# Softmax-weight transposes on VectorE and through DRAM in a fused attention and feed-forward kernel

## The chip, the cores and the metric

One core of one Trainium2 chip runs the whole program. The metric is device microseconds (us) of one execution, as the median of several runs.

## What is computed

The reference, cut to its arithmetic (q, k and v are 4 batches x 8 heads x 768 positions x 64, float32; n_sink = 4, window = 128; w_in is 512 x 2048, w_out 2048 x 512):

```
keep = (key < n_sink) | ((0 <= query - key) & (query - key < window))
scores = q @ k.T / 8, and -1e9 where not keep
a = exp(scores - rowmax); a = a / (sum(a) + 1e-9)
x = a @ v, heads put side by side: 3072 tokens x 512
h = x @ w_in; g = h - tanh(h); out = g @ w_out
```

## The kernel before

The 3072 tokens are cut into 12 chunks of 256 (three per batch). A chunk's attention is done in four **units**, one for each pair of heads, so there are 48 units, u = 0 to 47, and unit u belongs to chunk u // 4. A unit's steps, with the tile names that the profile shows:

- `split` (L471 on): ScalarE and VectorE cut keys and queries into a high and a low part (tiles `ks` and `q`). The first 12 units skip it.
- `scores` (L504 on), once for each half t of the chunk's 256 queries: four matmuls of 260 columns into tile `s` (L523). `s` has one buffer, so that the second half has to wait until VectorE has read the first (`merge`: L535 and L541), which writes the packed scores `p`. A query sees 4 sink keys and 128 keys of the band, so a row of `p` is 132 wide. ScalarE takes the exponential (L549).
- `normalise`: VectorE makes the reciprocal sums (L569, L570), ScalarE scales the four rows (L575), GpSimd copies out the sink columns (`z`).
- `turn` (L593 on): TensorE turns the four 128 x 128 blocks of weights (two heads by two halves) against the identity, into PSUM tile `t` (L602). VectorE multiplies them into tile `pt` twice, once by the mask `below` (keys of the query's own block) and once by `after` (keys of the block before): two operations over 512 columns at L616. In the first chunk of a batch they are 256 wide, and ScalarE makes a plain copy beside them (L609).
- `attend` (L625 on), once per chunk from chunk 3 on: TensorE turns the sink weights (L633), ScalarE copies them (`zr`), and 2 + 24 matmuls build `x`, the chunk's attention output, from `pt` and the values `v` (L650, L656). ScalarE and VectorE split `x` into `xh` and `xl`.

The feed-forward part has 96 **steps**: 12 chunks by 8 groups of 256 hidden columns. Step n is a block h(n) of 24 matmuls (L730), a gate on ScalarE and VectorE (tanh L735, difference L738, cast to `gh` L742, rest to `gl` L746), and a block o(n) of 12 matmuls (L778), 8 of them with `gh` and then 4 with `gl`. `h` has two PSUM buffers. The weights are loaded once, early, and decoded on VectorE and ScalarE (L165 to L169, L703, L708).

**What sets the order.** The engines run in the order in which `Work.order` (L216 on) lists the jobs. Each job has an engine, an estimated duration, a due time and the resources that it reads and writes. A list scheduler gives every engine, whenever it is free, the ready job that is due first. SyncE (SP), which issues the DMAs, is planned in the same way: one queue, in order. On TensorE `rank` bends this rule from step 23 on: a started block is finished first, and after an o block an h block goes ahead of anything else:

```python
if last[0] == "o":
    return (0 if b and b[0] == "h" else 1, due, n)
```

So attention work enters TensorE's order only behind an h block. The due time of a unit (`due_unit`) is that of its chunk's first step less `LEAD` = 24000 ns and less 14400 ns for each unit that follows it in the chunk; a gate is due with its step. The first matmul of an h block is written with a reordered access pattern where the block before it is not h (`_pieces`, L178: pieces of 16 elements).

Of the kernel before, what the change touches and what calls it, by code (L numbers as in the profile page):

```python
# [9 lines left out]
F32 = mybir.dt.float32  # L10
# [176 lines left out]
class Work:  # L187
# [28 lines left out]
    def order(self):  # L216
        todo = {}
        for n, (engine, *_) in enumerate(self.all):
            todo.setdefault(engine, []).append(n)
        users, left = [[] for _ in self.all], [len(t[4]) for t in self.all]  # L220
        for n, t in enumerate(self.all):
            for a in t[4]:
                users[a].append(n)
        ready = {n: 0.0 for n, k in enumerate(left) if k == 0}
        waiting = {e: [n for n in v if n in ready] for e, v in todo.items()}
        free, port, start, done = dict(self.BEGIN), {}, {}, {}
        parts, last = {}, None
        for b in self.block:
            parts[b] = parts.get(b, 0) + 1

        def rank(n):

            b, due = self.block[n], self.all[n][2]
            if last is None or last[1] < FREE or self.all[n][0] != "PE":
                return (1, due, n)
            if parts[last]:
                return (0 if b == last else 1, due, n)
            if last[0] == "o":
                return (0 if b and b[0] == "h" else 1, due, n)
            return (1, due, n)  # L240

        def at(n, e):
            t = max(free[e], ready[n])
            return max(t, port.get("DVE" if e == "POOL" else "POOL", 0.0)) if self.all[n][6] else t

        while any(waiting.values()):
            t, e = min((min(at(n, e) for n in v), e) for e, v in waiting.items() if v)
            n = min((n for n in waiting[e] if at(n, e) <= t), key=rank)
            if self.block[n]:
                last = self.block[n]  # L250
                parts[last] -= 1
            _, took, _, _, _, lands, locks = self.all[n]
            waiting[e].remove(n)
            start[n], free[e], done[n] = t, t + took, t + took
            if lands:
                free[e], done[n] = t + lands, t + lands + self.LANDING
            if locks:
                port[e] = t + took
            for u in users[n]:
                f = self.all[u][0]  # L260
                lag = 0 if f == e else self.WAKE[e] + (self.SLACK if f == "PE" else 0)
                ready[u] = max(ready.get(u, 0.0), done[n] + lag)
                left[u] -= 1
                if not left[u]:
                    waiting[f].append(u)
        return sorted(start, key=lambda n: (start[n], n)), start


def _banded(tc, qd, kp, vp, vs, masks, w_in, w_out, ident, pts, early, out):
    nc = tc.nc  # L270
    et = mybir.EngineType
    with ExitStack() as ctx:

        def pool(name, bufs, **kw):
            return ctx.enter_context(tc.tile_pool(name=name, bufs=bufs, **kw))
# [5 lines left out]
        qpool, vpool, hpool = pool("qpool", 2), pool("vpool", 3), pool("hpool", 1)  # L281
        xpool, gpool = pool("xpool", 2), pool("gpool", 2)
        spool, pp, sm = pool("spool", 1), pool("pp", 2), pool("sm", 4)
        ps_s, ps_t, ps_x = pool("ps_s", 1, space=PSUM), pool("ps_t", 1, space=PSUM), pool("ps_x", 1, space=PSUM)
        ps_h, ps_o = pool("ps_h", 2, space=PSUM), pool("ps_o", 1, space=PSUM)
        work, before = Work(), {}


        RAW, TWO, CUT, DUO, PB, ZL, TK = 12, 12, 1, 3, 4, 0, 1100

        chunks = [(b, 0) for b in range(3)] + [(b, c) for b in range(3) for c in range(1, CPB)]
        chunks += [(b, c) for b in range(3, B) for c in range(CPB)]
# [2 lines left out]
        order += [(cc, g) for g in range(CUT, NG) for cc in (2, 1)] + [(0, g) for g in range(CUT, NG)]  # L295
        order += [(cc, g) for cc in range(3, NCHUNK) for g in range(NG)]
        NS = len(order)
        FIRST, EARLY, PACE, LEAD = 55000.0, 4600.0, 7200.0, 24000.0
        UNIT, SECOND, WLEAD, WNEXT = 2600.0, 1000.0, 6000.0, 1500.0

        def due_step(n):
# [288 lines left out]
        def place(u):  # L590
            return u % 2 if u < DUO * NPAIR else u % NPAIR

        def turn(u):  # L593
# [28 lines left out]
            work.add("DVE", 430 if c == 0 else 710, d + 1500, lambda: part(1, below), ["t"], [("pt own", m)])  # L622
            work.add("DVE", 430 if c == 0 else 710, d + 1500, lambda: part(0, after), ["t"], [("pt before", m)])

        def attend(cc, p0, pairs):  # L625

            b, c = chunks[cc]
            key, banks = (cc, p0), range(pairs // 2)

            def sink_rows():  # L630
                xps[key] = [ps_x.tile([P, 2, CH], F32, tag="x", name=f"x{cc}_{p0}")]
                for t in range(2):
                    nc.tensor.transpose(  # L633
                        xps[key][0][:, 1, t * P : (t + 1) * P],
                        zt[:, t].bitcast(F32).rearrange("p n a b c -> p (n a b c)"), ident,
                    )

            def sink_copy(m):

                nc.scalar.activation(zr[:, m, :], xps[key][0][:, 1, :], AF.Copy, scale=odd[:, m : m + 1])  # L640

            def values():
                if pairs == NPAIR:
                    ps = ps_t.tile([P, 2, 2, P], F32, tag="t", name=f"x{cc}_2")
                    xps[key].append(ps.rearrange("p a b q -> p a (b q)"))
                plan = [(2 * c, 0, CH, 1), (2 * c + 1, P, CH, 3)]
                if c > 0:
                    plan.append((2 * c - 1, 0, P, 0))
                for i in banks:
                    nc.tensor.matmul(xps[key][i], lhsT=vsink[:, p0 // 2 + i], rhs=zr, start=True, stop=False)  # L650
                for p in range(p0, p0 + pairs):
                    for n, (i, a, z, blk) in enumerate(plan):
                        for h in range(2):
                            rhs = pts[:, place(NPAIR * cc + p), h].rearrange("p a b -> p (a b)")[:, blk * P : blk * P + z - a]
                            hd = (2 * p + h) * D
                            nc.tensor.matmul(  # L656
                                xps[key][(p - p0) // 2][h * 64 : h * 64 + 64, p % 2, a:z],
                                lhsT=vt[cc, i][:, hd : hd + D], rhs=rhs,
                                start=False, stop=p % 2 == 1 and n == len(plan) - 1,
                            )  # L660

            def x_high(i):
                if p0 == 0 and i == 0:
                    where, a, b = (hpool, "hb", "ha") if home(cc) == 2 else (xpool, "xh", "xl")
                    xh[cc] = where.tile([P, NPAIR, CH], F32R, tag=a, name=f"xh{cc}")
                    xl[cc] = where.tile([P, NPAIR, CH], F32R, tag=b, name=f"xl{cc}")
                r = slice(p0 + 2 * i, p0 + 2 * i + 2)
                nc.scalar.copy(xh[cc][:, r, :], xps[key][i])

            def x_low(i):  # L670
                r = slice(p0 + 2 * i, p0 + 2 * i + 2)
                nc.vector.tensor_tensor(xl[cc][:, r, :], xps[key][i], xh[cc][:, r, :].bitcast(F32), op=ALU.subtract)

            last = NPAIR * cc + p0 + pairs - 1
            d = due_unit(last) + 5500
            work.add("PE", 230, d + 1500, sink_rows, [("z", i) for i in range(NPAIR)], ["x"])
            for m in range(2):
                work.add("ACT", 270, d + 2000, lambda m=m: sink_copy(m), ["x"], [("zr", m)])
            v = [vslot[cc, i] for i in range(max(0, 2 * c - 1), 2 * c + 2)]
            pt = [(f"pt {k}", place(NPAIR * cc + i)) for k in ("whole", "own", "before") for i in range(p0, p0 + pairs)]  # L680
            need = pt + ["vsink", ("zr", 0), ("zr", 1)] + v
            work.add("PE", (340 + 735 * pairs if c == 0 else 200 + TK * pairs), d + 3500, values, need, ["x", "t"][: pairs // 2])
            for i in banks:
                x = [("xu", home(cc), p0 + 2 * i), ("xu", home(cc), p0 + 2 * i + 1)]
                work.add("ACT", 490, d + 5000, lambda i=i: x_high(i), ["xt"[i]], x + [("x", home(cc))] * (p0 + i == 0))
                work.add("DVE", 690, d + 5200, lambda i=i: x_low(i), ["xt"[i]], x)
# [45 lines left out]
        def gate(n):  # L732
# [12 lines left out]
                gl[n] = gpool.tile([P, 2, CH], F32R, tag="gl", name=f"gl{n}")  # L745
                nc.vector.tensor_tensor(gl[n], hps[n], gh[n].bitcast(F32), op=ALU.subtract)  # L746

            d, h, r = due_step(n), ("h", n % 2), n % 2
            work.add("ACT", 510, d, tanh, [h], ["gr"])
            work.add("DVE", 705, d, difference, ["gr"], [h])  # L750
            work.add("ACT", 526, d, high, [h], [("gh", r)])
# [80 lines left out]
        def attention(cc):  # L832
            if cc and chunks[cc][0] != chunks[cc - 1][0]:
                sink_values(chunks[cc][0], due_unit(NPAIR * cc) + 4000)
            for u in range(NPAIR * cc, NPAIR * cc + NPAIR):
                if not raw(u):
                    split(u)
                for t in range(2):
                    scores(u, t)
                if RAW <= u + 2 < NU:  # L840
                    load_qk(u + 2)
                normalise(u)
                turn(u)
                if cc < DUO and u % 2:
                    attend(cc, u % NPAIR - 1, 2)
            if cc >= DUO:
# [244 lines left out]
```

## Time and profile before

| | |
|---|---|
| three runs, median (lowest to highest) | 679.7 us (679.7 to 679.93) |
| the profiled execution's own time | 680.06 us |
| its span, first to last instruction | 678.3 us |
| busy: TensorE, VectorE, ScalarE, GpSimd | 664.6, 426.7, 368.0, 51.1 us |
| mean granted TensorE clock | 0.999 of full speed |

A busy time is the sum over the stretches in which the engine had at least one instruction under way. Matmuls overlap each other: the mean duration of one is longer than the distance from one start to the next, so the pace of TensorE is read from the starts. "Idle before" names the engine or the transfer whose end released the waiting instruction.

### The profile page before, as it was taken

To read this page: it belongs to the slowest core of one execution; us is meant where nothing else is said; L and a number is where in the kernel's file an instruction comes from. 1 tells how busy PE (TensorE), PEld (TensorE's weight loads), DVE (VectorE), ACT (ScalarE), POOL (GpSimd) and SP (SyncE) were. 2 spreads that over 40 slices of the span, in tenths; PEclk is the share of its full clock that TensorE was granted. 3 is DMA by queue.
4 is the path that set the end of the run, shared out by engine and by line. 5 is a ranking of instruction groups with operands and counts; after the bars stand their busy time and mean duration, and the time that the engine had idled before them with its cause. 6 is when DMAs were issued, how large, how long until landed. Compare 5 with 4: busy or idle time off the path is not lost.

```text
span 678.3 us, 12421 instructions
## 1 busy us (share of the span) xinstructions
PE 664.6 (98%) x4604; PEld 592.8 (87%) x4604; DVE 426.7 (63%) x1084; ACT 368.0 (54%) x1001; POOL 51.1 (8%) x201
## 2 busy tenths in 40 slices
PE   7999999999999999999999999999999999999996
PEld 5777899999989989989989998998998998998995
DVE  6889999947945556656655665565555656564221
ACT  5996433447845565455455655556556456553222
POOL 6220000000000010000001000001000000000000
PEclk9999999999999999999999999999999999999999
DMA  6789800012121022012103112112013102100001
GB/s 207 246 266 385 337 1 5 0 62 84 56 75 45 28 83 82 28 59 68 48 28 110 52 32 90 29 55 92 27 30 100 45 28 60 59 1 1 32 1 36
DMA packets 31712, 52.13 MB, mean 77 GB/s; under 512 B 3228, under 2 KB 21020, under 8 KB 31644
## 3 DMA queue, kind: packets, MB, share of 16 engines
q1 hardware_dynamic: 31340, 50.93, 22.8%
q8 instruction: 38, 0.62, 0.4%
q10 hardware_dynamic: 304, 0.33, 0.2%
q14 instruction: 30, 0.25, 0.1%
HBM read 44.96 MB, written 6.29 MB: 76 GB/s over the span
## 4 chain that ended last, share of the span: by engine, by line
PE 90%; ACT 3%; DVE 3%; SPq 1%; issue 1%; POOL 1%; DMA 1%; POOLq 0%; ACTq 0%
PE o L778 39%; PE h L730 37%; PE s L523 5%; PE x L656 5%; PE t L602 2%; ACT p L575 1%; ACT p L549 1%; PE x L650 1%; DMA qk<-kp 1%; DVE p L541 0%; DVE pt L167 0%; PE x L633 0%; DVE pt L169 0%; SPq L106 0%; DVE pt L616 0%
## 5 line engine op out<-in xcount | busy, mean ns | idle before, releaser
L730 PE MATMUL h<-xh,w 128*128 128x256 f32 x1536 | 279.9, 278 | 0.0
L730 PEld LDWEIGHTS h<-xh,w 128*128 128x128 f32 x1536 | 239.1, 188 | 3.3
L730 PE MATMUL h<-xl,w 128*128 128x256 f32 x768 | 212.5, 277 | 0.0
L778 PE MATMUL o<-w,gh 128*128 128x512 f32 x768 | 194.6, 394 | 0.6 <-ACT gh L742 0.6
L778 PEld LDWEIGHTS o<-w,gh 128*128 128x128 f32 x768 | 137.2, 188 | 26.4 <-ACT gh L742 1.0
L730 PEld LDWEIGHTS h<-xl,w 128*128 128x128 f32 x768 | 144.2, 188 | 3.2
L735 ACT ACTIVATE graw<-h 128x512 f32<-128x512 f32 x96 | 57.4, 598 | 157.5 <-PE h L730 157.2
L778 PE MATMUL o<-w,gl 128*128 128x512 f32 x384 | 103.9, 391 | 0.0
L549 ACT ACTIVATE p<-p,st 128x132 f32<-128x132 f32 x192 | 76.0, 398 | 48.3 <-DVE st L541 47.9
L746 DVE TENSOR_TENSOR gl<-h,gh 128x512 fp32r<-128x512 f32 x96 | 66.2, 690 | 46.7 <-ACT gh L742 46.5
L738 DVE TENSOR_TENSOR h<-h,graw 128x512 f32<-128x512 f32 x96 | 66.9, 696 | 40.5 <-ACT graw L735 39.4
L535 DVE COPY_PREDICATED s<-above,s 128x256 f32<-128x256 uint32 x80 | 33.9, 424 | 92.6 <-PE s L523 92.4
L778 PEld LDWEIGHTS o<-w,gl 128*128 128x128 f32 x384 | 71.7, 188 | 15.4
L742 ACT CAST gh<-h 128x512 fp32r<-128x512 f32 x96 | 56.2, 586 | 30.3 <-DVE h L738 30.2
L575 ACT ACTIVATE p<-p,st 128x132 f32<-128x132 f32 x192 | 62.1, 396 | 7.2 <-DVE st L570 7.0
L541 DVE CUSTOM_DVE_ANT_0 p<-s,mask 128x132 f32<-128x132 f32 x192 | 48.9, 292 | 8.2 <-POOL qraw L374 2.4
L523 PE MATMUL s<-ks,q 128*128 128x260 f32 x288 | 49.7, 295 | 0.0
L580 POOL CAST z<-p 128x16 fp32r<-128x16 f32 x48 | 10.2, 212 | 500.8 <-ACT p L575 498.9
L616 DVE TENSOR_TENSOR pt<-t,below 128x512 f32<-128x512 f32 (+1 forms) x48 | 28.8, 601 | 30.3 <-PE t L602 29.0
L485 DVE TENSOR_TENSOR ks<-kraw,ks 64x392 fp32r<-64x392 f32 x72 | 40.4, 561 | 5.7 <-ACT ks L480 3.5
L656 PE MATMUL x<-pt,v 128*64 128x128 f32 (+1 forms) x512 | 41.5, 315 | 0.0
L656 PEld LDWEIGHTS x<-pt,v 128*64 128x64 f32 x512 | 31.0, 137 | 11.7 <-issue 4.8
(77 smaller groups left out, 547.4 us busy)
## 6 DMA issues: line engine op xcount, KB each, us to landing
qraw<-qd SPq DMA_DIRECT2D x36, 256.0 KB, 2.7
wraw<-w_in SPq DMA_DIRECT2D x16, 512.0 KB, 7.2
wraw<-w_out SPq DMA_DIRECT2D x16, 512.0 KB, 8.2
kraw<-kp SPq DMA_DIRECT2D x37, 196.0 KB, 2.4
v<-vp SPq DMA_DIRECT2D x27, 256.0 KB, 2.7
out<-ob SPq DMA_DIRECT2D x24, 256.0 KB, 2.3
qk<-kp SPq DMA_DIRECT2D x8, 196.0 KB, 4.9
qk<-qd SPq DMA_DIRECT2D x16, 64.0 KB, 4.8
```

Of the source, the lines that this page charges most:

```text
L485: nc.vector.tensor_tensor(k[o, h, :], t[r, :], k[r, h, :].bitcast(F32), op=ALU.subtract)
L523: nc.tensor.matmul(ps[h][:, :WIN], lhsT=q[:, h, t * P : (t + 1) * P], rhs=rhs, start=i == 0, stop=i == 1,)
L541: nc.vector.tensor_tensor_reduce(out=pr[u][:, j, :], in0=ps[h][:, P:WIN], in1=mask[:, kind, :], scale=-0.125, scalar=BIG, op0=ALU.add, op1 ...
L549: nc.scalar.activation(e, e, AF.Exp, bias=st[u][:, j : j + 1], scale=-1.0, accum_out=st[u][:, 4 + j : 5 + j],)
L575: nc.scalar.activation(pr[u][:, j, :], pr[u][:, j, :], AF.Copy, scale=s[:, 8 + j : 9 + j])
L656: nc.tensor.matmul(xps[key][(p - p0) // 2][h * 64 : h * 64 + 64, p % 2, a:z], lhsT=vt[cc, i][:, hd : hd + D], rhs=rhs, start=False, stop=p ...
L730: nc.tensor.matmul(y, lhsT=w, rhs=x, start=r == 0, stop=r == 11)
L735: nc.scalar.activation(gr[n], hps[n], AF.Tanh)
L738: nc.vector.tensor_tensor(hps[n], hps[n], gr[n], op=ALU.subtract)
L742: nc.scalar.copy(gh[n], hps[n])
L746: nc.vector.tensor_tensor(gl[n], hps[n], gh[n].bitcast(F32), op=ALU.subtract)
L778: nc.tensor.matmul(ops[cc, t], lhsT=(gh, gh, gl)[i][n][:, f, t * P : (t + 1) * P], rhs=wt[1, g][:, (0, 1, 0)[i], f, :], start=first and no ...
```

## The change

From chunk 4 on (units 16 to 47; `APART` = 16) `turn_apart` takes the place of `turn`. VectorE transposes the four blocks in squares of 32 x 32 (`squares`) into one half of `pt`. SyncE writes that half, 128 rows of 2 KB, to a DRAM buffer (`away`) and reads it back in four transfers of 32 partitions, in runs of 512 bytes, so that each square comes to its place (`back`), into the other half of `pt`. VectorE then multiplies by `after` into the first half (`not_own`: two operations of 8 x 32 columns, one in the first chunk of a batch) and by `below` in place (`only_own`: 512 columns, or 256). `attend` reads the columns of `pt` through `weight_columns`, in runs of 32 elements that lie 128 elements apart. Units 0 to 15 keep the old way.

Three numbers of the planner change besides: the rule of `rank` that is quoted above goes away, so that attention may follow an o block as well; `LEAD` is 42000 ns in place of 24000; gates are due 12000 ns earlier from step 20 on.

```diff
-            if last[0] == "o":
-                return (0 if b and b[0] == "h" else 1, due, n)
+        dram = pool("dram", 4, space=bass.MemoryType.DRAM)
-        FIRST, EARLY, PACE, LEAD = 55000.0, 4600.0, 7200.0, 24000.0
+        FIRST, EARLY, PACE, LEAD = 55000.0, 4600.0, 7200.0, 42000.0
+        def weight_columns(m, h, blk):
+            v = pts[:, m].rearrange("p h b q -> p (h b q)").rearrange("p (r h t j) -> p r h t j", h=2, t=2, j=32)
+            return {1: v[:, :, h, 0], 3: v[:, :4, h, 1], 0: v[:, 4:, h, 1]}[blk]
+        def turn_apart(u):
...
+            def squares():
+                dst = other.rearrange("p b h t j -> p (h t) b j")
+                nc.vector.transpose(dst, pr[u][:, :, NSK:].rearrange("p n (b j) -> p n b j", j=32))
+            def away():
+                dt[0] = dram.tile([P, 4 * P], F32, tag="turned", name=f"turned{u}")
+                nc.sync.dma_start(dt[0], other.rearrange("p b h t j -> p (b h t j)"))
+            def back():
+                rows = dt[0].rearrange("(a i) (b e) -> b i a e", a=4, b=4)
+                dst = own.rearrange("p a h t j -> p a (h t j)")
+                for b in range(4):
+                    nc.sync.dma_start(dst[32 * b : 32 * b + 32], rows[b])
...
+            def not_own():
+                for t in range(c == 0, 2):
+                    masked(other[:, :, :, 1 - t], own[:, :, :, t], after)
+            def only_own():
+                v = own[:, :, :, 1] if c == 0 else own.rearrange("p a h t j -> p a (h t) j")
+                masked(v, v, below)
...
+            work.add("DVE", 620, d, squares, ps, before)
+            work.add("SP", 500, d + 800, away, before, [("turned", u % 4)], lands=800)
+            work.add("SP", 1500, d + 4200, back, [("turned", u % 4)], mine + [("pt whole", m)], lands=1500)
+            work.add("DVE", took if c == 0 else 760, d + 8000, not_own, mine, before, port=True)
+            work.add("DVE", took, d + 8000, only_own, (), mine, port=True)
...
+                            if NPAIR * cc + p >= APART:
+                                rhs = weight_columns(place(NPAIR * cc + p), h, blk)
...
-            d = due_unit(last) + 5500
+            d = due_unit(last) + (5500 if NPAIR * cc < APART else 9500)
...
-            d, h, r = due_step(n), ("h", n % 2), n % 2
+            d, h, r = due_step(n) - (12000.0 if n >= 20 else 0.0), ("h", n % 2), n % 2
...
-                turn(u)
+                (turn if u < APART else turn_apart)(u)
```

**TensorE, around step 42 or 43, before.** L602 are the transposes, L523 the scores, L778 an o block, L730 the first matmuls of the next h block:

```order
L602 MATMUL t<-ident,p 128x128 x4
L523 MATMUL s_0<-ks,q 128x260 x4
L778 MATMUL o<-w_2,gh 128x512 x8
L778 MATMUL o<-w_2,gl 128x512 x4
L730 MATMUL h<-xh,w_4 128x4x4x16
```

**TensorE there with the change.** Line numbers are those of the changed file: L522 scores, L687 the turned sink rows, L834 o, L786 h:

```order
L522 MATMUL s_0<-ks,q 128x260 x4
L687 MATMUL x_0<-ident,z 128x128 x2
L834 MATMUL o<-w_3,gh 128x512 x8
L834 MATMUL o<-w_3,gl 128x512 x4
L522 MATMUL s_1<-ks,q 128x260 x4
L834 MATMUL o<-w_4,gh 128x512 x8
L834 MATMUL o<-w_4,gl 128x512 x4
L786 MATMUL h<-xh,w_5 128x4x4x16
```

The transposes are gone. Before, each o block was followed by an h block, and the two halves of a unit's scores had an h and an o block between them; now they stand one o block apart, o(43) and o(44) follow each other with only scores between them, and h(43) and h(44) stood together ahead of them.

**VectorE, around one unit, before.** L738 and L746 are the gate's difference and `gl`, L616 the two masked copies out of PSUM, L535 and the ISA rows the merge of the scores:

```order
L738 TENSOR_TENSOR h<-h,graw 128x512
L746 TENSOR_TENSOR gl<-h,gh 128x512
L616 TENSOR_TENSOR pt<-t,below 128x4x128
L616 TENSOR_TENSOR pt<-t,after 128x4x128
L535 COPY_PREDICATED s_0<-above,s_0 128x2x128
L541 ISA p,st<-s_0,mask 128x132
```

**VectorE around one unit with the change.** L492 and L484 are the low parts of queries and keys, L659 the masks, L794 and L802 the gate, L644 the squares:

```order
L492 TENSOR_TENSOR q<-qraw,q 128x512
L659 TENSOR_TENSOR pt<-pt,after 128x8x32 x2
L659 TENSOR_TENSOR pt<-pt,below 128x512
L568 TENSOR_SCALAR st<-st 128x4
L569 RECIPROCAL st<-st 128x4
L484 TENSOR_TENSOR ks<-kraw,ks 64x392
L794 TENSOR_TENSOR h<-h,graw 128x512
L484 TENSOR_TENSOR ks<-kraw,ks 64x392
L644 STREAM_TRANSPOSE pt<-p 128x4x4x32
L802 TENSOR_TENSOR gl<-h,gh 128x512
```

The masks of one unit stand ahead of the squares of the next, and both stand in the queue that the gate's difference and `gl` use.

**SyncE around one chunk's end, with the change.** L648 is `away`, L654 `back`, L851 the store of the output, L365 and L354 the loads of queries and keys:

```order
L648 DMA turned<-pt 128x512
L654 DMA pt<-turned 32x4x128 x4
L851 DMA out<-ob_0 128x512
L851 DMA out<-ob_1 128x512
L365 DMA qraw<-qd 128x2x256
L354 DMA kraw<-kp 128x392
L648 DMA turned<-pt 128x512
L654 DMA pt<-turned 32x4x128 x4
```

Before, the queue held only the loads and the stores there. Each unit now puts a write and four reads between them, the reads waiting for the write.

## Rows read from the trace of the kernel before

**Rows 1.** Busy time in stretches: us, PE, PEld, DVE, ACT, POOL, clock, DMA share, GB/s.

```profile
85.00:102.00 17.00, 17.00 (x115) 15.53 (x113) 16.86 (x20) 6.53 (x10) 0.00 (x0) 1.00 0.00 1
...
221.00:238.00 17.00, 17.00 (x114) 15.48 (x114) 10.34 (x31) 9.52 (x27) 0.63 (x3) 1.00 0.09 28
```

**Rows 2.** TensorE's waits over the span: us in total, times, longest us.

```profile
PE o L778 <- ACT gh L742: 0.6, 2, 0.3
```

**Rows 3.** TensorE's timeline: start us, us, line, operation, count.

```profile
201.16 0.28 PE L730 MATMUL h<-xh,w 128*128 128x256 f32 x1
201.27 0.28 PE L730 MATMUL h<-xl,w 128*128 128x256 f32 x1
...
203.90 0.64 PE L523 MATMUL s<-ks,q 128*128 128x260 f32 x4
204.38 2.02 PE L778 MATMUL o<-w,gh 128*128 128x512 f32 x8
...
215.87 0.60 PE L602 MATMUL t<-ident,p 128*128 128x128 f32 x4
216.23 0.73 PE L523 MATMUL s<-ks,q 128*128 128x260 f32 x4
216.80 2.00 PE L778 MATMUL o<-w,gh 128*128 128x512 f32 x8
...
240.68 0.60 PE L602 MATMUL t<-ident,p 128*128 128x128 f32 x4
241.11 0.38 PE L633 MATMUL x<-ident,z 128*128 128x128 f32 x2
241.25 0.72 PE L523 MATMUL s<-ks,q 128*128 128x260 f32 x4
241.81 2.01 PE L778 MATMUL o<-w,gh 128*128 128x512 f32 x8
...
245.12 3.69 PE L656 MATMUL x<-pt,v 128*64 128x256 f32 x48
```

**Rows 4.** Groups by shape: count | busy us, mean ns of one | idle before.

```profile
L602 PE MATMUL t<-ident,p 128*128 128x128 f32 x192 | 29.4, 275 | 2.5 <-DVE pt L616 1.2 <-ACT p L575 0.8 <-ACT pt L609 0.4
L616 DVE TENSOR_TENSOR pt<-t,below 128x512 f32<-128x512 f32 x32 | 22.1, 691 | 26.5 <-PE t L602 26.5
```

**Rows 5.** Timeline of TensorE and ScalarE, one half of a unit: scores, then the scaled rows.

```profile
263.96 0.64 PE L523 MATMUL s<-ks,q 128*128 128x260 f32 x4
...
267.32 1.30 ACT L575 ACTIVATE p<-p,st 128x132 f32<-128x132 f32 x4 [0.25 <-DVE st L570]
```

**Rows 6.** DMA issues by tile: count, KB each, median us to landing; and the queue's line.

```profile
q1 hardware_dynamic: 31340, 50.93, 22.8%
...
qraw<-qd SPq DMA_DIRECT2D x36, 256.0 KB, 2.7
...
out<-ob SPq DMA_DIRECT2D x24, 256.0 KB, 2.3
```

**Rows 7.** SyncE's timeline of the early stretch: start us, us, line, transfer, count.

```profile
66.46 2.86 SPq L401 DMA_DIRECT2D v<-vp  x3
```

**Rows 8.** VectorE's timeline, the first decoding operation of w_in's group 5.

```profile
100.81 0.69 DVE L165 TENSOR_SCALAR pt<-wraw 128x1024 uint32<-128x1024 uint32 x1
```

**Rows 9.** The chain that ended last, two h blocks (88, 89) and o(88).

```profile
629.00 5.46 PE h L730 x48
634.47 2.74 PE o L778 x12
```

**Rows 10.** ScalarE's timeline, the gate of step 88: tanh, then `gh`.

```profile
631.84 0.60 ACT L735 ACTIVATE graw<-h 128x512 f32<-128x512 f32 x1 [1.73 <-PE h L730]
633.21 0.59 ACT L742 CAST gh<-h 128x512 fp32r<-128x512 f32 x1 [0.77 <-DVE h L738]
```

**Rows 11.** Timelines of TensorE and ScalarE, step 41: h(41) ends with L602's start; `gh`.

```profile
257.55 0.60 PE L602 MATMUL t<-ident,p 128*128 128x128 f32 x4
...
261.04 0.57 ACT L742 CAST gh<-h 128x512 fp32r<-128x512 f32 x1
```

More of the change, by code (lines that the diff above doesn't have):

```diff
@@ L286, in _banded @@
         work, before = Work(), {}
-        RAW, TWO, CUT, DUO, PB, ZL, TK = 12, 12, 1, 3, 4, 0, 1100
+        RAW, TWO, CUT, DUO, PB, ZL, TK, APART = 12, 12, 1, 3, 4, 0, 1100, 16
         chunks = [(b, 0) for b in range(3)] + [(b, c) for b in range(3) for c in range(1, CPB)]
@@ L623, in turn, with halves @@
             work.add("DVE", 430 if c == 0 else 710, d + 1500, lambda: part(0, after), ["t"], [("pt before", m)])
+        def halves(m):
+            v = pts[:, m].rearrange("p h b q -> p (h b q)").rearrange("p (o a h t j) -> p o a h t j", o=2, a=4, h=2, t=2)
+            return v[:, 1], v[:, 0]
+        def weight_columns(m, h, blk):
+            v = pts[:, m].rearrange("p h b q -> p (h b q)").rearrange("p (r h t j) -> p r h t j", h=2, t=2, j=32)
+            return {1: v[:, :, h, 0], 3: v[:, :4, h, 1], 0: v[:, 4:, h, 1]}[blk]
@@ new lines, in turn_apart, with masked @@
+        def turn_apart(u):
+            cc, p, b, c = unit(u)
+            m = place(u)
+            other, own = halves(m)
+            dt = {}
+            def squares():
[9 more added lines that the diff above has]
+                    nc.sync.dma_start(dst[32 * b : 32 * b + 32], rows[b])
+            def masked(dst, src, mask):
+                z = list(src.shape)
+                mask = mask.rearrange("p (a j) -> p a j", j=32).unsqueeze(2).to_broadcast(z)
+                nc.vector.tensor_tensor(dst, src, mask, op=ALU.mult)
+            def not_own():
[4 more added lines that the diff above has]
+                masked(v, v, below)
+            d = due_unit(u) + 5500
+            ps = [("p", slot(u), 0), ("p", slot(u), 1)]
+            took = 430 if c == 0 else 710
+            before, mine = [("pt before", m)], [("pt own", m)]
+            work.add("DVE", 620, d, squares, ps, before)
[3 more added lines that the diff above has]
+            work.add("DVE", took, d + 8000, only_own, (), mine, port=True)
```

## The prediction

> **What bounds the kernel now.** I read the busy time by stretches first. From 85 us on TensorE is busy for all 17.00 us of every 17, and its clock is granted in full (1.00) [rows 1]. The other engines are not full in the steady part: VectorE has 10.34 and ScalarE 9.52 of 17 us. VectorE is full only early (16.86 of 17 at 85 to 102 us), while it decodes weights [rows 1]. The list of TensorE's waits says the same from the other side: for the gate's result `gh` it waited 0.6 us in the whole run, in two places [rows 2]. So after the start the time is the sum of TensorE's blocks, and what leaves TensorE leaves the time, unless a new wait comes in. The price of a block is read in TensorE's timeline, as the distance from its start to the next start [rows 3].
>
> **What the change takes off TensorE.** Units 16 to 47 lose their transposes: 32 units, four each. Four transposes start at 215.87 us and the scores behind them at 216.23, so 0.36 us. They also make the next block slower: those scores take 216.80 - 216.23 = 0.57, where scores behind an h block take 204.38 - 203.90 = 0.48. A unit thus loses 0.36 + 0.09 = 0.45 us [rows 3]. In eight of the 32, one per chunk, the turned sink rows (L633) stand between transposes and scores. These sink rows stay, are the same kind of matmul and keep the slower block behind them, so only about 0.36 goes. The stretch there, from 240.68 to 241.81, is 1.13 us for the three [rows 3]. Sum: 24 x 0.45 + 8 x 0.36 = **13.7 us**.
>
> The mean duration of a transpose in the list of groups is 275 ns [rows 4], and 128 of them would be 35.2 us. That is the wrong column: they overlap, and four take 0.36 us from start to start. The Trainium skill (TensorE: Matmul & The Clock Gate, "Part 4: PE-mode transpose") gives about 275 ns for a transpose in a kernel's context and 390 ns alone. By that figure the saving would again be an estimated 35 us, and the pace in this trace contradicts it.
>
> **What it adds to TensorE.** The 24 matmuls of each x block now read weights in runs of 32 elements. The trace has a nearer case than the plain one: the first matmul of an h block reads pieces of 16 elements and starts its successor after 201.27 - 201.16 = 0.11 us, the pace of a plain one [rows 3]. I take 0. The other end would be half pace in all eight x blocks, 8 x 3.6 = 29 us (the block of 48 passes from 245.12) [rows 3].
>
> **VectorE.** Two masked operations per unit, 691 ns each [rows 4], become squares, one or two half-wide masks and one full mask. None of these shows in the trace. The nearest row is the same 691 ns for 512 columns, and I take that for each 512: three in place of two, 0.7 us more per unit and 32 x 0.7 = 22 us in about 450. That raises 10.34 of 17 to about 11.2 [rows 1]. VectorE does not become the bound. If the squares cost twice as much, it is 11.9. At the low end masks out of SBUF are cheaper and the load stays as it is. ScalarE loses four plain copies.
>
> **SyncE and the DMAs.** Each unit adds one write of 256 KB and four reads of 64 KB. The page's queue line gives 22.8% of 16 engines over 678.3 us for 31340 packets, 79 ns a packet [rows 6]. A unit adds 128 packets of 2 KB and 512 of 512 bytes, so 640 x 0.079 / 16 = 3.2 us of DMA time, against about 13 us between units (eight steps of 5.5 us and the attention blocks make a chunk of over 50): cover enough. The nearest write, `out`, lands in 2.3 us, and a read of as many bytes (`qraw`) in 2.7 [rows 6]. For the four reads the ends are 2.7 (side by side) and 10.8 (one after the other). Three issues in a row took 2.86 us at most [rows 7], so the last of four is issued no more than about 2.9 us after the first, and 2.7 + 2.9 = 5.6 bounds them if they overlap. I take 4.2, nearer to side by side.
>
> The in-order queue is also moved early on: loads for chunk 3 (`kraw`, `qraw`, `vraw`, three `v`) now stand ahead of the weight groups 4 and 5. The `v` loads wait for a buffer until 66.46 us and end at 69.32 [rows 7], so group 5 starts behind them. VectorE first needs it at 100.81 [rows 8], 31 us later, more than ten times what a load of 256 KB takes [rows 6]. That costs nothing.
>
> **Is x ready in time?** With the changed order I count the blocks on TensorE between a chunk's last scores and its x block: 17.6 us in five chunks, 16.6 in one, 14.9 in two (h and o 2.74 each, scores 0.48) [rows 3, 9]. What has to fit: scores end to scaled weights, 264.4 to 268.6, is 4.2 us with its queueing [rows 5]; squares 0.7; write 2.3; reads 4.2; masks 1.4; some five handoffs of 0.1. Sum 13.3 us, 14.7 with the reads at 5.6. It fits, with little to spare in two chunks.
>
> **Are the gates ready in time?** This is where I expect what the change gives back. Before, an h and an o block, 5.5 us or more, nearly always lay between the end of h(n) and the start of o(n). In the changed order I count 34 steps from 27 to 87 with only 2.74 to 4.15 us. A gate with nothing in its way takes from 631.73 (h(88) ends halfway through 5.46 us from 629.00) to 633.80 (the end of `gh`), 2.1 us, and 2.2 with the handoff [rows 9, 10]; its 2.74 us of cover were enough. A gate in a full queue took much longer: h(41) ended at 257.55 and its `gh` at 261.61, 4.1 us [rows 11]. Over the counted steps, waits sum to 0 us if a gate needs 2.2 us, 1.7 at 3.2, 7.3 at 3.5 and 22.3 at 4.1. I take 0.8, a need of about 3.0. The planner puts o(n) where its own estimate has the gate done, and the order that it made from the same estimates before, in which x blocks too were placed as soon as they were due, left TensorE waiting 0.6 us for `gh` [rows 2].
>
> **Sum.** 680.06 - 13.7 + 0.8 = 667.2 us against the profiled execution's own time (span 678.3 to 665.4). That execution is 0.36 above the median of 679.7, so the forecast is **666.8 us**.
>
> **The rivals.**
> - *The gates wait a little* (a need of 3.5 us): 679.7 - 13.7 + 7.3 = 673.3. For it: three VectorE operations more stand in the gate's queue, and the scores' merges must fit behind a single o block. Against: the earlier due times put gates ahead. Chance 0.19.
> - *The gates wait as at step 41*, slower than before. Place: o(n) directly behind the previous o block. Price: 679.7 - 13.7 + 22.3 = 688.3. It turns the sign from a mean need of about 3.75 us on. Against: at step 41 the planner had 5.5 us or more and no reason to hurry. Chance 0.06.
> - *The round trip is late.* If the four reads land one after the other (10.8 us), the chain is 19.9 us, and x waits 5 x 2.3 + 3.3 + 2 x 5.0 = 24.8 us: 690.8. It turns the sign from reads of about 9 us on. Against: 16 engines share the packets. Chance 0.05. The Trainium skill (VectorE: DVE Perf Modes, "The three transpose paths") warns that a plain copy which transposes by its strides is 19 times slower than the DMA's own transpose where the innermost step is large. By that factor the reads would take an estimated 80 us, and x would hold every chunk. Here the innermost run is 512 bytes long, not a single element, and no row before shows such a copy.
> - *Runs of 32 halve TensorE's pace*: 679.7 - 13.7 + 29 = 695.0, chance 0.03, with the 0.11 us against it [rows 3].
> - *The listed mean is what leaves*: 679.7 - 35.2 = 644.5, chance 0.01.
> - *Nothing is left*: the waits happen to take about what the transposes gave. Chance 0.02.
>
> The forecast itself, with waits of up to 4 us (665.6 to 670), keeps 0.64.
>
> **Range and chances.** A measurement of this kernel tells about 0.2%, 1.4 us. The range goes from 664.8 (0.45 us saved at the eight sink places too, 14.4 in all, and scores that follow an o block a little cheaper) up to 675, past the first rival; the slower cases, 0.14 together, are left out, with the few others. Faster: 0.64 + 0.19 + 0.01 = 0.84; same 0.02; slower 0.14.
>
> **What would show it.** L602 falls from 192 to 64 matmuls and the stretches from 200 us on stay at 17.00 of 17, with chunks about 1.7 us shorter than before. TensorE's waits show at most a few microseconds for `gh` or for `s`, and none for `pt`. The squares and masks last 0.4 to 0.8 us each, and VectorE stays near 11 of 17. The reads land within about 4 us. I am wrong if TensorE has holes behind o blocks (the gate), ahead of x (the round trip) or behind the first half of the scores (the merge), or if the x block takes more than 3.7 us.

## The result, and the profile after

The changed kernel takes 667.83 us (median of four runs, beside 679.79 us for the kernel before): a ratio of 0.9822, 95% interval 0.9803 to 0.9841. One of the four runs took 1319.9 us, which no other run here came near, and is left out of the ratio; the other three took 667.43 to 668.03 us. The forecast was 666.8 us, in a range of 664.8 to 675. The profiled execution took 667.43 us, its span is 665.7 us, 12.6 less than before.

The page after, busy times (us, share of the span, instructions):

```profile
PE 652.5 (98%) x4476; PEld 580.9 (87%) x4476; DVE 450.8 (68%) x1144; ACT 367.3 (55%) x997; POOL 54.7 (8%) x201
```

Busy time by stretches after, columns as in [rows 1]:

```profile
85.00:102.00 17.00, 17.00 (x115) 15.53 (x114) 16.11 (x21) 6.43 (x9) 0.00 (x0) 1.00 0.11 36
...
221.00:238.00 17.00, 17.00 (x117) 15.57 (x115) 12.21 (x35) 10.43 (x32) 1.75 (x6) 1.00 0.30 86
```

TensorE is still full in every one of the stretches of 17 us that I read between 85 and 646 us. VectorE has 12.21 of 17 us in the stretch from 221 us, and 11.30 in the mean of those stretches, where it had 10.50 before. TensorE's wait for `gh` in the list of waits, then the same two waits in its timeline:

```profile
PE o L834 <- ACT gh L798: 0.6, 2, 0.3
```

```profile
60.82 1.20 PE L834 MATMUL o<-w,gh 128*128 128x512 f32 x4 [0.30 <-ACT gh L798]
...
70.85 1.43 PE L834 MATMUL o<-w,gh 128*128 128x512 f32 x5 [0.31 <-ACT gh L798]
```

They are the two early waits of before [rows 2]. In the 34 steps with little cover, the list shows no wait at all.

The changed operations, groups by shape after (L601 is the old transpose, L644 the squares, L659 the masks):

```profile
L659 DVE TENSOR_TENSOR pt<-pt,after 128x256 f32<-128x256 f32 x60 | 22.9, 421 | 5.4 <-DMA pt<-turned 4.6 <-DVE st L540 0.3
L644 DVE STREAM_TRANSPOSE pt<-p 128x512 f32<-128x512 f32 x32 | 22.6, 707 | 4.8 <-ACT p L574 4.6
...
L659 DVE TENSOR_TENSOR pt<-pt,below 128x512 f32<-128x512 f32 x28 | 19.3, 691 | 0.8
...
L601 PE MATMUL t<-ident,p 128*128 128x128 f32 x64 | 10.2, 279 | 2.7 <-DVE pt L615 1.3 <-ACT p L574 1.1 <-ACT pt L608 0.3
```

The squares take 707 ns where I took 691 [rows 4]. The full mask takes the 691 that I took, a half-wide one 421 where half of 691 would be 346. In three places VectorE waited for the reads ahead of the masks, 4.6 us in all; TensorE waited at none of them. The round trip, among the DMA issues after (count, KB each, median us to landing):

```profile
turned<-pt SPq DMA_DIRECT2D x32, 256.0 KB, 2.4
pt<-turned SPq DMA_DIRECT2D x128, 64.0 KB, 2.0
```

**Where TensorE's time went.** I added up the distances between the starts of its blocks, from the sink products ahead of the x block of chunk 3 (188 us) to the start of the last o block but one:

| | before | after |
|---|---|---|
| transposes t | 12.0 | 0 |
| scores s | 33.0 | 30.0 |
| o blocks | 198.8 | 199.4 |
| h blocks | 197.5 | 199.6 |
| x, its sink rows and their products | 37.8 | 37.9 |
| sum | 479.05 | 466.93 |

So 12.12 us of the 12.6 left here. The rest is 0.13 ahead of this stretch and 0.4 behind it. The row of the h blocks is the surprise: they grew by 2.1 us, though there are as many of them and they waited for nothing. The chain after shows it at the pairs of h blocks that the new order makes:

```profile
322.45 5.65 PE h L786 x48
...
334.82 5.46 PE h L786 x48
```

Both are 48 matmuls with no gap. Before, such a pair took 5.46 or 5.47 throughout [rows 9]. The slow pairs stand behind an o block and scores, the quick ones directly behind an o block. From the x block of chunk 3 on, 32 h blocks stand behind an o block and scores, singly or in pairs, and 29 of them are slow (2.82 us, or 5.65 for two together). The other three, single ones, are not, though the two blocks ahead of them are the same:

```profile
307.28 2.74 PE h L786 x24
```

So what stood further back has a part in it as well.

### The profile page after: what moved, and what is told of

Its sections match the earlier page's. It is cut to its first block, busy times and chain, and to the rows that moved or that the text cites. A ratio compares the mean times of both kernels' runs of the same rounds, so it can differ in the third digit from the quotient of the medians.

```text
span 665.7 us, 12542 instructions
## 1 busy us (share of the span) xinstructions
PE 652.5 (98%) x4476; PEld 580.9 (87%) x4476; DVE 450.8 (68%) x1144; ACT 367.3 (55%) x997; POOL 54.7 (8%) x201
## 4 chain that ended last, share of the span: by engine, by line
PE 89%; DVE 3%; ACT 3%; DMA 2%; issue 1%; POOL 1%; SPq 0%; POOLq 0%; DVEq 0%
PE o L834 39%; PE h L786 38%; PE s L522 5%; PE x L712 5%; DMA wraw<-w_out 2%; ACT p L548 1%; ACT p L574 1%; PE x L704 1%; DVE p L540 0%; DVE pt L167 0%; PE x L687 0%; DVE pt L169 0%; DVE pt L615 0%; SPq L411 0%; PE s L515 0%
## 5 line engine op out<-in xcount | busy, mean ns | idle before, releaser
L786 PE MATMUL h<-xh,w 128*128 128x256 f32 x1536 | 279.9, 279 | 0.0
L786 PEld LDWEIGHTS h<-xh,w 128*128 128x128 f32 x1536 | 239.2, 188 | 2.1
L786 PE MATMUL h<-xl,w 128*128 128x256 f32 x768 | 213.5, 278 | 0.0
L834 PE MATMUL o<-w,gh 128*128 128x512 f32 x768 | 195.3, 395 | 0.6 <-ACT gh L798 0.6
L834 PEld LDWEIGHTS o<-w,gh 128*128 128x128 f32 x768 | 137.3, 188 | 27.3 <-issue 1.4
L786 PEld LDWEIGHTS h<-xl,w 128*128 128x128 f32 x768 | 144.3, 188 | 2.0
L794 DVE TENSOR_TENSOR h<-h,graw 128x512 f32<-128x512 f32 x96 | 66.8, 695 | 72.1 <-ACT graw L791 71.8
L834 PE MATMUL o<-w,gl 128*128 128x512 f32 x384 | 103.8, 390 | 0.0
L802 DVE TENSOR_TENSOR gl<-h,gh 128x512 fp32r<-128x512 f32 x96 | 65.6, 684 | 31.0 <-ACT gh L798 30.8
L834 PEld LDWEIGHTS o<-w,gl 128*128 128x128 f32 x384 | 71.7, 188 | 15.0
L579 POOL CAST z<-p 128x16 fp32r<-128x16 f32 x48 | 12.9, 268 | 488.8 <-ACT p L574 486.9
L522 PE MATMUL s<-ks,q 128*128 128x260 f32 x288 | 46.7, 284 | 0.0
L522 PEld LDWEIGHTS s<-ks,q 128*128 128x128 f32 x288 | 41.9, 188 | 3.9 <-issue 0.5
L484 DVE TENSOR_TENSOR ks<-kraw,ks 64x392 fp32r<-64x392 f32 x72 | 40.4, 562 | 2.3
```

The lines of the kernel that those rows point to most:

```text
L484: nc.vector.tensor_tensor(k[o, h, :], t[r, :], k[r, h, :].bitcast(F32), op=ALU.subtract)
L522: nc.tensor.matmul(ps[h][:, :WIN], lhsT=q[:, h, t * P : (t + 1) * P], rhs=rhs, start=i == 0, stop=i == 1,)
L786: nc.tensor.matmul(y, lhsT=w, rhs=x, start=r == 0, stop=r == 11)
L794: nc.vector.tensor_tensor(hps[n], hps[n], gr[n], op=ALU.subtract)
L834: nc.tensor.matmul(ops[cc, t], lhsT=(gh, gh, gl)[i][n][:, f, t * P : (t + 1) * P], rhs=wt[1, g][:, (0, 1, 0)[i], f, :], start=first and no ...
```

## The experiments

### The planner's numbers alone, and the new transposes alone

```diff
 e1_order_alone: the kernel before, and
-            if last[0] == "o":
-                return (0 if b and b[0] == "h" else 1, due, n)
-        FIRST, EARLY, PACE, LEAD = 55000.0, 4600.0, 7200.0, 24000.0
+        FIRST, EARLY, PACE, LEAD = 55000.0, 4600.0, 7200.0, 42000.0
-            d, h, r = due_step(n), ("h", n % 2), n % 2
+            d, h, r = due_step(n) - (12000.0 if n >= 20 else 0.0), ("h", n % 2), n % 2

 e2_turn_alone: the changed kernel with these three lines as they were before
```

> The old transposes with only the three numbers of the planner changed (no rule after o, lead 42000, gates due 12000 earlier). Theory: the gain is the transposes that leave TensorE, and the freer order costs about 0.08 us for each h block that starts behind o and scores (2.74 to 2.82 us); the order has 39 such blocks, so 679.8 + 3.2 = about 683 us, with L602's 192 matmuls as before and no new waits. Rival: the longer lead and the freer order themselves give part of the gain: 679 us or less.

Measured: 683.8 us against 679.8 (ratio 1.006, 1.0043 to 1.0077). The order by itself costs 4.0 us. No wait above 0.2 us is added, and the pairs of h blocks are slow all along its chain (the last row here is a single block):

```profile
206.83 5.65 PE h L728 x48
219.38 5.65 PE h L728 x48
236.44 5.65 PE h L728 x48
...
258.31 2.74 PE h L728 x24
```

In the sums of blocks h is 201.5 us, 4.0 more than before, and the other rows nearly cancel. So the cost is that of slower h blocks, as the theory has it, but its places are right only in part. Of the 39 blocks that it counted behind o and scores, the 32 in pairs are slow, at 0.19 us a pair. The seven single ones stay at 2.74, as in the last row. Seven pairs behind x and scores, which it had not counted, are slow too (236.44).

> The new transposes alone, with the rule after o, the lead of 24000 and the gates' due times of before. No h block stands behind o and scores. Theory: TensorE loses the transposes and pays nothing for the order, 679.8 - 14.3 - 0.4 = about 665 us, if x is in time. Rival: the lead is what hides the round trip. The order leaves only 12.5 us between a chunk's last scores and its x block, where the changed kernel has 14.8 to 17.5 and one chunk's chain took 14.5: x then waits about 1 to 2 us in each of eight chunks, 673 to 681 us, and TensorE shows waits ahead of L656's counterpart.

Measured: 685.6 us (1.0086, 1.0069 to 1.0102): slower than before, by more than the rival had said. TensorE's list of waits (us in total, times, longest):

```profile
PE h L788 <- DVE xl L730: 11.3, 8, 1.6
...
PE o L836 <- ACT gh L800: 2.2, 7, 0.5
```

The wait is not where I had put it. The x block itself starts without one; what is late is its split. TensorE's timeline of this kernel at chunk 4:

```profile
248.70 3.69 PE L714 MATMUL x<-pt,v 128*64 128x256 f32 x48
252.33 0.74 PE L524 MATMUL s<-ks,q 128*128 128x260 f32 x4
252.91 0.28 PE L788 MATMUL h<-xh,w 128*128 128x256 f32 x1
254.75 0.39 PE L788 MATMUL h<-xl,w 128*128 128x256 f32 x1 [1.56 <-DVE xl L730]
```

The order leaves one block of scores, 0.5 us, between the end of x and the first h block of its chunk, so `xl`, which VectorE makes from x, is not there. In the order before, 3.3 us lay between them in seven of the eight chunks, and in the changed kernel 6.7 to 12.1. In the planner's terms x is due 4 us later than before (9500 ns in place of 5500), to leave room for the round trip, and with the old lead that takes away the time for the split. The longer lead gives it back, and neither half of the change is a gain without the other. In the sums of blocks of this kernel h is 210.9 us, 13.4 more than before, of which 11.3 are these waits.

### The rule after o, put back

```diff
 e3_rank_kept: the changed kernel, and
+            if last[0] == "o":
+                return (0 if b and b[0] == "h" else 1, due, n)
```

> The changed kernel with the rule after o put back (lead 42000 and gates' due times as changed). One h block in place of 32 stands behind o and scores. Theory: h blocks return to 2.74 us and the time falls by about 2.2 us, to 665.6. Rival: the freedom to follow o is needed to have x and the gates in time (x stands only 12.5 us behind its scores in one chunk): no gain, 668 us or more, with waits.

Measured: 673.25 us (0.9902, 0.9886 to 0.9919). My theory fell here, at least as a sum. The h blocks do return to 2.74 us, but waits more than eat it:

```profile
PE s L524 <- DVE st L542: 2.6, 2, 1.3
PE o L836 <- ACT gh L800: 1.9, 5, 0.5
PE h L788 <- DVE xl L730: 1.6, 1, 1.6
```

These three make 6.1 us, of which 0.6 are the early waits for `gh`. With places for attention only behind h, x again ended only 0.6 us ahead of its first h block in one chunk, and h waited there for `xl`. So the freedom to follow o is worth more than the slower h blocks cost: 5.4 us between the two medians.

### The slow h blocks

```diff
 e4_plain_first: the changed kernel, and
-            if k == 0 and before["h", n] != "h":
+            if k == 0 and before["h", n] == "o":

 e8_first_score: the changed kernel, and in the scores' products
-                    rhs = ks[u][:, h, t * TS : t * TS + WIN]
                     for i, q in enumerate((qh[u], ql[u])):
+                        rhs, y = ks[u][:, h, t * TS : t * TS + WIN], ps[h][:, :WIN]
+                        if h == 0 and i == 0 and kind_before[0] == "o":
+                            rhs, y = _pieces(rhs, 5, 26), _pieces(y, 5, 26)
                         nc.tensor.matmul(
-                            ps[h][:, :WIN], lhsT=q[:, h, t * P : (t + 1) * P], rhs=rhs,
+                            y, lhsT=q[:, h, t * P : (t + 1) * P], rhs=rhs,
```

(`kind_before` holds "o" where the block ahead on TensorE is an o block.)

> The changed kernel, but the first matmul of an h block is written with the reordered pattern only directly behind an o block, and plainly behind scores or x. Theory A: an h block that starts behind o and scores is slow whatever its first pattern is: 667.8 us as the changed kernel. Theory B: the reordered first matmul behind scores sets the slow pace: h blocks return to 2.74 us, 665.6 us.

Measured: 667.81 us (0.9823, 0.9806 to 0.9839), the changed kernel's time. Theory A holds: behind o and scores it does not matter how the h block's own first matmul is written. Behind an h block and scores it does. The changed kernel has three h blocks there, and this kernel writes their first matmul plainly; first the changed kernel's row, then this one's:

```profile
295.34 2.74 PE h L786 x24
```

```profile
295.65 2.83 PE h L786 x24
```

> The changed kernel, but the first matmul of a block of scores that stands directly behind an o block reads and writes in a reordered pattern (pieces of 26), as the first of an h block does there. Theory: the slow pace starts at the step from o to the scores and is carried through them into h, so the reordered first score ends it: h blocks behind o and scores return to 2.74 us, 667.8 - 2.2 = 665.6 us. Rival: the pace comes from the scores themselves or from something else in that order: h stays at 2.82 and 5.65 us, 667.8 us.

Measured: 665.93 us (0.9795, 0.9779 to 0.9812); its runs lie between 665.69 and 666.1, those of the changed kernel between 667.43 and 668.03. The same pair of h blocks at the same place in the chain, first the changed kernel's row, then this one's:

```profile
245.87 5.65 PE h L786 x48
```

```profile
245.87 5.46 PE h L788 x48
```

The sum of its h blocks is 197.2 us, where the changed kernel has 199.6 and the one before 197.5. One matmul of the scores, read and written in pieces, changes the pace of the 24 or 48 matmuls that come three matmuls later. It does not always make them quicker. The 29 slow blocks behind o and scores become quick, but the three that were quick there become slow, such as the one shown above at 307.28:

```profile
306.88 2.83 PE h L788 x24
```

Of the kernels here this is the quickest.

### How much cover the round trip and VectorE have

```diff
 e5_second_trip: the changed kernel, and at the end of back()
+                again = dram.tile([P, 4 * P], F32, tag="again", name=f"again{u}")
+                flat = own.rearrange("p a h t j -> p (a h t j)")
+                nc.sync.dma_start(again, flat)
+                nc.sync.dma_start(flat, again)

 e6_squares_twice: the changed kernel, and in squares()
-                nc.vector.transpose(dst, ...)
+                for _ in range(2):
+                    nc.vector.transpose(dst, ...)
```

> The changed kernel, in which each unit's weights make a second trip behind the first (written to DRAM again in one transfer and read back in one), which the planner does not know of: about 2.0 + 2.7 = 4.7 us more before the masks. Theory: the round trip is covered, but by little, since in chunk 5 the reads landed about 2 us before VectorE came to the masks and x stood 0.5 us behind the masks: x or the gates behind the late masks wait 2 to 3 us in each of eight chunks, 684 to 692 us. Rival: the cover is ample, and the trip's length does not matter: 670 us or less.

Measured: 743.86 us (1.0941, 1.0912 to 1.0969). The direction is the theory's, the size is not: far more than x waiting in eight chunks. Its waits, VectorE's masks first, then TensorE's:

```profile
DVE pt L663 <- DMA pt<-again: 99.9, 28, 8.2
```

```profile
PE o L838 <- ACT gh L802: 24.3, 16, 4.0
PE s L522 <- DVE ks L484: 16.0, 11, 3.6
```

I had the price per chunk, and it is per unit: 28 masks wait in VectorE's in-order queue, and the gates and score operands behind them wait with them, not x. Late loads are not the cause: none of VectorE's or ScalarE's waits in the steady part is for `qraw` or `kraw`. From 188 us on, TensorE's waits sum to 46 us of the 75 that the span is longer. TensorE is then no longer full, and its granted clock, 1.00 where it is full, is 0.80 over a stretch with gaps. A shorter stretch, behind a wait of 2.65 us for `ks`, has the lower of its two levels alone (0.50), and its h matmuls start 0.21 us apart where they start 0.11 to 0.12 apart elsewhere. By the granted clock of all the stretches, some 41 us of the span pass at that level. Half of that, about 20 us, is an estimate of what the clock cost:

```profile
236.50:239.50 3.00, 3.00 (x14) 3.00 (x15) 2.17 (x7) 1.93 (x8) 0.63 (x3) 0.50 0.49 154
...
323.00:340.00 17.00, 17.00 (x115) 15.57 (x115) 10.34 (x28) 11.17 (x32) 1.44 (x6) 1.00 0.43 130
476.00:493.00 17.00, 13.42 (x66) 11.24 (x66) 10.35 (x30) 10.05 (x30) 1.26 (x6) 0.80 0.36 116
```

```profile
236.42 0.77 PE L522 MATMUL s<-ks,q 128*128 128x260 f32 x2 [2.65 <-DVE ks L484]
236.99 0.41 PE L790 MATMUL h<-xh,w 128*128 128x256 f32 x1
237.20 0.42 PE L790 MATMUL h<-xl,w 128*128 128x256 f32 x1
```

> The changed kernel with the squares done twice on VectorE, unknown to the planner: 32 x 0.71 = 22.7 us more of its time. Theory: VectorE is no bound (11.1 of 17 us), and the second squares cost only where a gate stands behind them: 668 to 673 us. Rival: VectorE's queue sets the gates' end, and most of it comes through: 680 us or more.

Measured: 668.63 us (0.9834, 0.9814 to 0.9854), 0.8 us over the changed kernel for 22.8 us more work on VectorE; the two intervals overlap, so the 0.8 is not clear of noise. Its group of squares:

```profile
L645 DVE STREAM_TRANSPOSE pt<-p 128x512 f32<-128x512 f32 x64 | 45.4, 709 | 6.1 <-ACT p L574 4.8
```

So VectorE's own work is covered. A few short waits at the head of its queue were covered too (4.6 us in the changed kernel), but not the 99.9 us of the second trip.

### The remaining settings

```diff
 e7_chunk3: the changed kernel with APART = 12
 e9_lead_24: the changed kernel with LEAD = 24000.0
 e10_gates_due: the changed kernel, and
-            d, h, r = due_step(n) - (12000.0 if n >= 20 else 0.0), ("h", n % 2), n % 2
+            d, h, r = due_step(n), ("h", n % 2), n % 2
```

> The changed kernel with chunk 3 (units 12 to 15) turned the new way as well. Theory: what leaves TensorE leaves the time, 4 x 0.45 us less transposes, and three more h blocks behind o and scores at 0.08: 667.8 - 1.8 + 0.2 = 666.2 us. Rival: VectorE, fuller there after decoding the weights, makes gates or x late: 668 us or more.

Measured: 669.5 us (0.9845, 0.9828 to 0.9861), 1.7 us slower than the changed kernel where I had forecast 1.6 quicker. TensorE stops being full in a stretch where the changed kernel has 17.00 of 17 (the changed kernel's row, then this one's):

```profile
170.00:187.00 17.00, 17.00 (x121) 15.72 (x121) 15.63 (x47) 13.92 (x43) 1.25 (x6) 1.00 0.21 55
```

```profile
170.00:187.00 17.00, 15.99 (x108) 14.27 (x107) 15.13 (x44) 11.91 (x37) 1.44 (x6) 1.00 0.44 133
```

Its waits for `gh` are 2.0 us in all, 1.4 more than in the changed kernel. The rest of the 3.3 us between forecast and result I did not trace to rows.

> The changed kernel with the lead back at 24000 (attention may follow o, gates due 12000 earlier). In its order x ends 2.7 us ahead of its chunk's first h block in most chunks, 1.0 in one and 0.0 in the last, where the changed kernel has 6.4 to 11.9. Theory: what the lead buys is the time in which x is split into xh and xl (about 1.9 us were wanted where the new transposes stood alone): h waits for xl by about 1 and 2 us in two chunks, and with 50 steps of little cover in place of 34 the gates cost 1 to 3 us: 670 to 673 us. Rival: once attention may follow o, the lead buys nothing: 668.5 us or less.

Measured: 670.32 us (0.9862, 0.9833 to 0.989), as forecast, but not by the mechanism that I gave: h waits for `xl` 0.3 us only, and the scores carry more (32.6 us in the sum, where the changed kernel has 30.0). Of that, 1.3 us is one wait of the scores for VectorE's merge, which the changed kernel does not have:

```profile
PE s L522 <- DVE st L540: 1.3, 1, 1.3
```

The lead is worth some 2.5 us once attention may follow o.

> The changed kernel with the gates due with their steps as before. TensorE's order is nearly that of the changed kernel (36 steps with little cover in place of 34). Theory: the earlier due times only keep the gates ahead of attention in the queues of VectorE and ScalarE; the planner lays TensorE's order around the later gates, and little changes: 667.5 to 669.5 us. Rival: without them gates stand behind masks and merges, and o blocks wait for gh: 672 us or more.

Measured: 668.63 us (0.9837, 0.9808 to 0.9865), 0.8 over the changed kernel, with 0.4 us more wait for `gh`. The difference is not clear of noise, so the gates' due times are a detail.

## Why the prediction was right

- **What leaves TensorE leaves the time.** Right. TensorE stays full, and 12.1 of the 12.6 us are found in its blocks.
- **13.7 us for the transposes.** The transposes took 12.01 us and the slower scores behind them 2.97. Of that, 0.75 came back in o blocks, x and its products, since the o block now often stands behind x or the sink rows, where the scores stood. That makes 14.2, so I was 0.5 short. The mean of 275 ns in the groups, 35.2 us in all, would have been far off, and with it the sum that the Trainium skill's figure gives (TensorE: Matmul & The Clock Gate, "Part 4: PE-mode transpose").
- **Nothing added on TensorE.** For the x blocks this held: 3.62 us for 48 matmuls before and after, so runs of 32 elements cost nothing (the chain before, then after):

```profile
245.18 3.62 PE x L656 x48
```

```profile
285.54 3.62 PE x L712 x48
```

For the order it did not hold: I priced every h block at 2.74 us wherever it stood. The 29 slow ones behind o and scores cost 0.09 more each, and the row of the h blocks grew by 2.1 us. This term was missing from the sum.
- **0.8 us of waits at the gates.** There were none after the start. Where the cover was thin, down to 2.74 us, the gates took less. Three errors, 0.5 and 0.8 one way and 2.1 the other, nearly cancel: 13.7 - 0.8 = 12.9 forecast, 14.2 - 2.1 = 12.1 measured. That the sum came closer than its terms is luck.
- **The round trip.** In chunk 5, after, VectorE's squares, SyncE's transfers, VectorE's masks and TensorE's x (one fence for each engine):

```profile
274.70 0.71 DVE L644 STREAM_TRANSPOSE pt<-p 128x512 f32<-128x512 f32 x1 [0.45 <-ACT p L574]
...
282.85 0.76 DVE L659 TENSOR_TENSOR pt<-pt,after 128x256 f32<-128x256 f32 x2
283.64 0.69 DVE L659 TENSOR_TENSOR pt<-pt,below 128x512 f32<-128x512 f32 x1
```

```profile
275.44 0.33 SPq L648 DMA_DIRECT2D turned<-pt  x1
277.47 1.75 SPq L654 DMA_DIRECT2D pt<-turned  x4
```

```profile
284.92 0.63 PE L704 MATMUL x<-zr,vsink 128*128 128x512 f32 x2
```

The write holds the queue 2.0 us, the four reads are issued within 1.75 and land 2.0 us after an issue, so they are in by about 281.2: 3.8 us where I took 4.2. The Trainium skill (VectorE: DVE Perf Modes, "The three transpose paths") states its factor of 19 against the DMA's own transpose, which no run here shows. Nothing like the estimated 80 us of that rival appears with runs of 512 bytes. The masks end at 284.33 and x starts 0.6 us later, so "it fits, with little to spare" was right. I had the rival wrong in its place, though: the second trip shows that a late read stops VectorE's queue, long before it stops x.

## What to carry to other kernels

Where one engine is full, price what leaves it by the distance from start to start, not by the mean duration. Then see whether the new order puts its blocks behind others than before, since a block's pace can depend on what stood two blocks ahead, or further back. A detour through DRAM cost next to nothing here because the order left room for it at every place that waits: the longer lead and the freer order cost 4 us by themselves, and the transposes without them 6, and together they gave 12. A transfer that an in-order engine waits for holds up everything behind it, so its cover is to be counted at that engine's queue.

## What was not expected of the hardware

A series of 128 x 256 matmuls (the h block) runs at 2.74 us for 24 or at 2.82, with no gap in either, and keeps its pace over 48. Which one it is depends on the blocks ahead and on how their first matmuls are written. Directly behind an o block it is 2.74 to 2.76 in the changed kernel, or 5.46 for two. Behind o and plainly written scores it is 2.82 in 29 places and 2.74 in three. With the first matmul of these scores in pieces of 26 elements each of these places has the other pace. The first matmul of the h block itself, in pieces or plain, changes nothing there, but behind an h block and scores it decides between 2.74 and 2.83. What in TensorE keeps that state, and which earlier block sets it, is not shown by these rows.
